# A 96-row weight load cut into fourteen loads of falling row counts, at the end of a decode kernel

## The chip, the cores and the metric

The kernel runs on one core of one Trainium2 chip. The metric is the device time of one execution in microseconds (us); lower is better. Three timed runs of the kernel before gave 190.89, 191.10 and 191.25 us; the median is 191.1 us.

## The reference, cut to what matters

One token (a row of 512 numbers) goes through two branches, which a gate then mixes. Branch A is attention with 32 heads over a cache of 4,096 keys and values. Branch B is a small dense network, whose second weight matrix is `w2` with 1,376 rows of 512 numbers.

```
h   = x @ w1 + b1                  # 512 -> 1376
h   = relu(h) ** 2
b   = h @ w2 + b2                  # 1376 -> 512; w2 is [1376, 512], bf16
a   = attention(x @ wq, k_cache, v_cache) @ wo
out = g * a + (1 - g) * b          # g = sigmoid(sum(x * gate_w))
```

The change concerns only how the last 96 of the 1,376 rows of `w2` (1376 = 10 * 128 + 96) come from device memory.

## The kernel before, in words

**Loads.** Nearly all loads are issued on one queue, that of SyncE (SP), in an order written out by hand in `ORDER` and the loop that starts at L265. The 32 heads are taken four at a time, so keys and values come as eight loads each of 4 MB (`load_kv`, L230). The last values load (V7) comes in four parts of 1 MB, each with a semaphore of its own. Between them stand `wq` (L223), `w1` (L273), four parts of `wo` (`load_wo`, L250, 1 MB each), and the five parts of `w2` (`load_w2`, L258). `W2_PARTS` (L65) names the five parts: two of four groups of 128 rows (512 KB each), then the rest of 96 rows (96 KB), then two of one group of 128 rows (128 KB each). The first part is issued ahead of V7. The other four stand at the very end of the queue, behind the last part of `wo`, in the order L277 to L280: the second four groups, the 96 rows, a group, a group. A DMA of up to 128 rows is spread over the core's 16 DMA engines, which each work through their own share of the queue in order. A DMA adds 16 to its semaphore in all.

**Where the rows go.** The 96 rows land in their own tile `w2b` (L104), the 1,280 others in `w2a` (L100). Until the last head group's scores are done, `w2a` also serves as the scratch tile of the products on VectorE, which is why the first part waits at L267.

**The end on TensorE.** After the last values have landed, TensorE runs this order, which L631 to L642 write out: the first part of `w2` (`mlp_out(0)`, L633), the transposes of the last attention rows (`turn`, `spread`), the last part of `wo` (`out_rows(1)`, L636), and then `mlp_out(1)` to `mlp_out(4)`. Each `mlp_out(c)` first waits for its part's semaphore (L535) and then issues four matmuls for every group of rows. All add into the same accumulator `acc`. Then VectorE adds the bias (L752), TensorE transposes (L642), VectorE copies (L754), and SP stores the 1 KB result with a DMA of four rows (L282), for which L757 waits. ScalarE issues four small loads at the start (L322 to L325): `x`, `gate_w` and `b1` as one row each, and `b2` as four rows.

Of the kernel before, what the change touches and what calls it, by code (L numbers as in the profile page):

```python
# [5 lines left out]
def bass_gated_mix__gqa_block_cached__dense_activation_squared_relu__decode_kernel(  # L6
# [24 lines left out]
    F = 1376  # L31
    FG = 10
# [29 lines left out]
    V_SLOT = [2 + q % 2 for q in range(NQ)]  # L62
    V_PARTS = [[4]] * (NQ - 1) + [[1, 1, 1, 1]]
    QF = 4
    W2_PARTS = [(0, 4), (4, 8), (FG, FG + 1), (8, 9), (9, 10)]  # L65


# [12 lines left out]
    with ctx:  # L80
        def sb(name, shape, dt):
            return ctx.enter_context(nc.sbuf_tensor(name, shape, dt))
# [4 lines left out]
        def sem(name):  # L87
            return ctx.enter_context(nc.semaphore(name))
# [15 lines left out]
        w2b = sb("w2b", [FR, DM], bf16)  # L104
# [49 lines left out]
        acc4 = pO[0:4, 128:192].bitcast(bf16)  # L154
        QR = [pQ[:, :]] + [p[:, :].bitcast(fp32) for p in KP[0:3]] + [pQ[:, :]] * (NQ - QF)
        H = KP[0][:, 0:2 * (FG + 1)].bitcast(fp32)
# [7 lines left out]
        s_w1 = sem("s_w1")  # L164
        s_w2 = [sem(f"s_w2{n}") for n in range(len(W2_PARTS))]
        s_wo = [sem(f"s_wo{g}") for g in range(2)]
# [61 lines left out]
        @block.sync  # L228
        def _(eng):
            def load_kv(n):  # L230
                kind, q = ORDER[n]
                if q >= 2:
                    done(kind, q - 2)
                if kind == "K":
                    eng.dma_start(KV[:, K_SLOT[q], :], k_q[q, :, :]).then_inc(s_k[q], 16)
                else:
                    at = 0
                    for m, sv in zip(V_PARTS[q], s_v[q]):
                        a, b = at * PB * 128, (at + m) * PB * 128
                        eng.dma_start(KV[:, V_SLOT[q], a:b], v_q[q, :, a:b]).then_inc(sv, 16)  # L240
                        at += m

            def done(kind, q):
                if kind == "K":
                    eng.wait_ge(s_sd, NP * (q + 1))
                    eng.wait_ge(s_t, GQ * (q + 1))
                else:
                    eng.wait_ge(s_pv, q + 1)

            def load_wo(g):  # L250
                if g == 0:
                    eng.wait_ge(s_qps, NQ)
                elif g < NG - 1:
                    eng.wait_ge(s_wd, g)
                a = 0 if g < NG - 1 else 1
                eng.dma_start(wo_sb[:, a, :, :], wo_v[g, :, :, :]).then_inc(s_wo[a], 16)

            def load_w2(n):  # L258
                a, b = W2_PARTS[n]
                if a < FG:  # L260
                    eng.dma_start(w2a[:, a:b, :], w2_v[:, a:b, :]).then_inc(s_w2[n], 16)
                else:
                    eng.dma_start(w2b[:, :], B_w2[FG * 128:F, :]).then_inc(s_w2[n], 16)

            for n in range(len(ORDER)):  # L265
                if n == len(ORDER) - 1:
                    eng.wait_ge(s_sd, NP * NQ)  # L267
                    load_w2(0)
                load_kv(n)
                if n == 2:  # L270
                    eng.wait_ge(s_z, 1)
                    eng.wait_ge(s_b2, 1)
                    eng.dma_start(w1_sb[:, :, :], w1_v[:, :, :]).then_inc(s_w1, 16)  # L273
                if n in WO_AT:
                    load_wo(WO_AT[n])
            load_wo(NG - 1)
            load_w2(1)  # L277
            load_w2(2)
            load_w2(3)
            load_w2(4)  # L280
            eng.wait_ge(s_f4, 1)
            eng.dma_start(out[0, 0, :].rearrange("(j p) -> j p", p=128), fin4[:, :]).then_inc(s_out, 16)  # L282
# [38 lines left out]
        def _(eng):  # L321
# [9 lines left out]
            def qb_copy(c):  # L331
                eng.wait_ge(s_qps, c + 1)
                for r in range(R):
                    eng.activation(qb[rows(r), c, :], QR[c][rows(r), r * 128:(r + 1) * 128], ACT.Copy)\  # L334
                       .then_inc(s_qb, 1)

            def qcol_copy(c):
                eng.wait_ge(s_q, c + 1)
                eng.activation(qcol[:, 4 * c:4 * c + 4], QR[c][:, 0:4], ACT.Copy).then_inc(s_qc, 1)
# [37 lines left out]

            for c in range(QF):
                qb_copy(c)
            for c in range(QF):  # L380
                qcol_copy(c)
# [22 lines left out]
        def _(eng):  # L404
# [32 lines left out]
            def q_rows(c):  # L437
                if c >= QF:
                    eng.wait_ge(s_qc, c)
                for t in range(4):  # L440
                    mm = eng.matmul(QR[c], xb[:, t, :], wq_sb[:, t, c * 512:(c + 1) * 512],  # L441
                                    start=(t == 0), stop=(t == 3))
                mm.then_inc(s_qps, 1)

            def q_cols(c):
                eng.wait_ge(s_qb, R * (c + 1))
                eng.matmul(QR[c][:, 0:4], qb[:, c, :], ident[:, 0:128:32], start=True, stop=True).then_inc(s_q, 1)
# [84 lines left out]
                mm.then_inc(s_wd, 1)  # L532

            def mlp_out(c, last=False):
                eng.wait_ge(s_w2[c], 16)  # L535
                a, b = W2_PARTS[c]
                for n in range(a, b):
                    M = 128 if n < FG else FR
                    w = w2a[:, n, :] if n < FG else w2b[:, :]
                    for j in range(4):  # L540
                        mm = eng.matmul(acc[:, j:j + 1], w[:, j * 128:(j + 1) * 128], hs[0:M, n:n + 1],  # L541
                                        start=False, stop=last, skip_group_check=True)
                if last:
                    mm.then_inc(s_acc, 1)
# [48 lines left out]
            eng.wait_ge(s_xb, 4)  # L593
            for c in range(QF):
                q_rows(c)
            for c in range(QF):
                q_cols(c)
# [33 lines left out]
            at("end")  # L631
            eng.wait_ge(s_hs, 2)
            mlp_out(0)  # L633
            turn()
            spread()
            out_rows(1)  # L636
            mlp_out(1)
            mlp_out(2)
            mlp_out(3)
            mlp_out(4, last=True)  # L640
# [145 lines left out]
```

## Time and profile before

| what | value |
|---|---|
| timed runs | 190.89, 191.10, 191.25 us; median 191.1 |
| the profiled execution's own time | 190.93 us |
| its span (first to last instruction) | 189.6 us |
| around the span | 1.3 us |
| TensorE busy | 138.7 us (73%) |
| VectorE busy | 123.0 us (65%) |
| ScalarE busy | 115.9 us (61%) |
| bytes moved by DMA, mean rate | 78.47 MB, 414 GB/s |
| share of the SP queue's packets in the time of 16 DMA engines | 97.1% |
| granted TensorE clock, mean | 0.725 (0.50 from 164 us to the end) |

How to read it: the span is the time from the first to the last instruction of the profiled execution, and the time of an execution is a little longer. An engine's busy time is a share of the whole span, and says little about one stage. For this change the last 8 us matter, in which the last loads land and TensorE adds them up. A packet is one DMA engine's move of one contiguous row; a 4-byte packet behind a load's rows is that engine's step of the load's semaphore.

### The profile page before, as it was taken

The numbers are of one execution on the slowest core, as the hardware profiler recorded it, in microseconds if no ns is written. First come the engines' busy times: TensorE is split into PE (matmuls) and PEld (weight loads), VectorE is DVE, ScalarE is ACT, GpSimd is POOL, SyncE is SP. The second block draws the span as 40 slices with busy tenths as digits, with TensorE's granted clock in tenths as the row PEclk, the third lists the DMA queues.
The fourth block names the chain that finished last, engine by engine and source line by source line (L and its number), as shares of the span: only waits on it lengthen the run. The fifth ranks groups of instructions, "written<-read, shape, count | busy, mean of one in ns | idle before, by whom it ended". The sixth has DMA issues, their size and how long they took to land. (4 is left out here: it accounts for less than half of the span.)

```text
span 189.6 us, 6235 instructions
## 1 busy us (share of the span) xinstructions
PE 138.7 (73%) x2688; PEld 120.8 (64%) x2688; DVE 123.0 (65%) x123; ACT 115.9 (61%) x242; POOL 6.0 (3%) x13
## 2 busy tenths in 40 slices
PE   0009587668849979969968797929867596899855
PEld 0003265536739779959958695829766595789854
DVE  1100099979969999996997299819990599701011
ACT  3004659948989985985987099709962298560000
POOL 4000000000700000000000000000000000000000
PEclk9999969958975965795795569555975589555555
DMA  6999999989999999999999999999999999999991
GB/s 218 443 443 442 443 442 425 429 374 481 425 387 422 442 443 439 430 436 429 429 430 422 422 429 436 442 443 442 404 446 429 422 411 432 444 387 422 420 389 62
DMA packets 4321, 78.47 MB, mean 414 GB/s; under 512 B 499, under 2 KB 853, under 8 KB 1110
## 3 DMA queue, kind: packets, MB, share of 16 engines
q1 hardware_dynamic: 4296, 78.32, 97.1%
q8 instruction: 7, 0.11, 0.2%
q14 instruction: 4, 0.03, 0.0%
q10 hardware_dynamic: 14, 0.01, 0.0%
HBM read 78.32 MB, written 0.00 MB: 413 GB/s over the span
## 5 line engine op out<-in xcount | busy, mean ns | idle before, releaser
L351 ACT ACTIVATE kT<-KP 128x1024 bf16<-128x1024 bf16 x80 | 75.4, 1041 | 25.2 <-PE KP L456 25.0
L681 DVE TENSOR_TENSOR w2a<-KV,qb 128x1536 f32<-128x1536 bf16 x32 | 56.3, 1760 | 18.3 <-DMA KV<-in_A_k_cache_dram 18.0
L456 PE MATMUL KP<-ident,KV 128*128 128x128 bf16 x640 | 60.0, 256 | 9.2 <-PEq L451 9.1
L456 PEld LDWEIGHTS KP<-ident,KV 128*128 128x128 bf16 x640 | 48.9, 117 | 12.6 <-issue 11.7
L685 DVE TENSOR_REDUCE S<-w2a 128x12 f32<-128x1536 f32 x32 | 56.1, 1753 | 1.1
L463 PE MATMUL pS<-qc,kT 128*128 128x4 bf16 x640 | 28.0, 166 | 13.0 <-PEq L451 11.2
L463 PEld LDWEIGHTS pS<-qc,kT 128*128 128x128 bf16 x640 | 24.7, 99 | 18.6 <-issue 17.3
L497 PEld LDWEIGHTS pO<-E,KV 128*128 128x128 bf16 x1024 | 29.4, 105 | 1.5 <-issue 1.5
L497 PE MATMUL pO<-E,KV 128*128 128x4 bf16 x1024 | 28.5, 166 | 1.4 <-PEq L451 1.4
L368 ACT ACTIVATE E<-S,nM 32x128 bf16<-32x128 f32 x32 | 18.5, 579 | 0.9
L441 PE MATMUL pQ<-W,xb 128*128 128x512 bf16 x20 | 7.8, 531 | 12.5 <-DMA W<-in_A_wq_dram 11.4
L334 ACT ACTIVATE qb<-pQ 32x128 bf16<-32x128 f32 x20 | 5.4, 268 | 14.2 <-PE pQ L441 13.9
L441 PEld LDWEIGHTS pQ<-W,xb 128*128 128x128 bf16 x20 | 2.2, 125 | 14.9 <-DMA W<-in_A_wq_dram 11.5
L357 ACT ACTIVATE S<-pS 32x80 f32<-32x80 f32 x32 | 7.3, 228 | 4.8 <-PE pS L463 4.2
L660 DVE TENSOR_SCALAR e<-ez 128x1 f32<-128x1 f32 x1 | 0.2, 154 | 14.1 <-ACT ez L383 14.1
L368 ACT ACTIVATION_READ_ACCUMULATOR E<-S,nM 32x1 f32 x32 | 8.1, 252 | 0.0
L704 DVE RECIPROCAL rden<-pO 128x4 f32<-128x4 f32 x8 | 1.4, 174 | 9.8 <-PE pO L497 9.8
L493 PE MATMUL pO<-RS,onesf 128*128 128x4 f32 x16 | 4.3, 339 | 1.8 <-PEq L451 1.8
L484 PE MATMUL pM<-identf,mp 128*1 128x128 f32 x8 | 3.0, 372 | 3.2 <-PEq L451 2.9
L493 PEld LDWEIGHTS pO<-RS,onesf 128*128 128x128 f32 x16 | 3.8, 297 | 2.1 <-issue 2.0
L441 PE MATMUL KP<-W,xb 128*128 128x512 bf16 x12 | 4.9, 591 | 0.0
L718 DVE TENSOR_SCALAR hr<-KP 128x10 f32<-128x10 f32 x1 | 0.2, 170 | 6.8 <-PE KP L509 6.8
(74 smaller groups left out, 70.1 us busy)
## 6 DMA issues: line engine op xcount, KB each, us to landing
KV<-in_A_k_cache_dram SPq DMA_DIRECT2D x8, 4096.0 KB, 22.1
KV<-in_A_v_cache_dram SPq DMA_DIRECT2D x7, 4096.0 KB, 28.9
W<-in_A_wq_dram SPq DMA_DIRECT2D x1, 4096.0 KB, 13.6
W<-in_A_wo_dram SPq DMA_DIRECT2D x4, 1024.0 KB, 17.2
KV<-in_A_v_cache_dram SPq DMA_DIRECT2D x4, 1024.0 KB, 13.2
w_sb<-in_B_w_dram SPq DMA_DIRECT2D x1, 1376.0 KB, 23.6
w2a<-in_B_w_dram SPq DMA_DIRECT2D x2, 512.0 KB, 13.9
w2a<-in_B_w_dram SPq DMA_DIRECT2D x2, 128.0 KB, 18.7
```

What stands on the lines that cost most here:

```text
L334: eng.activation(qb[rows(r), c, :], QR[c][rows(r), r * 128:(r + 1) * 128], ACT.Copy)\
L351: eng.activation(kT[:, n % NT, :], KP[n % NKP][:, :], ACT.Copy).then_inc(s_ev, 1)
L357: eng.activation(S[rows(r), q % NS, 0:YQ], S2[rows(r), :, r], ACT.Copy).then_inc(s_cp, 1)
L368: eng.activation(E[rows(r), q % 2, :, r], S[rows(r), q % NS, :], ACT.Exp, bias=nM[rows(r), q:q + 1], scale=SCALE, accum_out=RS[rows(r), q ...
L441: mm = eng.matmul(QR[c], xb[:, t, :], wq_sb[:, t, c * 512:(c + 1) * 512], start=(t == 0), stop=(t == 3))
L456: mm = eng.transpose(KP[(GQ * a + g) % NKP][:, y * 128:(y + 1) * 128], key(a, b), ident[:, :])
L463: mm = eng.matmul(pS[:, R * c:R * c + R], kT[:, (GQ * a + g) % NT, y * 128:(y + 1) * 128], qc2[:, a, :], start=True, stop=True)
L484: eng.transpose(MT, mp[:, a:a + 1], identf[:, :]).then_inc(s_mt, 1)
L493: eng.matmul(DEN[a], onesf[:, :], RS[:, a, :], start=True, stop=True)
L497: mm = eng.matmul(O[a], KV[:, V_SLOT[a], b * 128:(b + 1) * 128], E[:, a, COLUMN[b], :], start=(b == 0), stop=(b == NB - 1))
L681: eng.tensor_tensor(prod, KV[:, K_SLOT[q], x:x + XB * 128].rearrange("p (b d) -> p b d", d=128), qb[:, q, :].unsqueeze(1).to_broadcast([12 ...
L685: eng.tensor_reduce(S[:, q % NS, c:c + XB], prod, AX.X, ALU.add).then_inc(s_sd, 1)
```

## The change

`load_w2(2)` issued one load of 96 rows. It now issues fourteen, of 13, 12, 11, 10, 9, 8, 7, 6, 5, 4, 3, 2, 1 and 5 rows, one behind the other on the same queue, at the same place in its order. All add to the same semaphore, and the wait on TensorE ahead of the four matmuls of `w2b` goes from 16 to 16 * 14 = 224. The rows, their bytes and their place in `w2b` stay the same; nothing else is edited. In the order of instructions, only SP's list grows (by 13 DMAs, between the second and the fourth part of `w2`); those of the other engines are the same.

```diff
+    W2B_PARTS = list(range(13, 0, -1)) + [5]
     W2_PARTS = [(0, 4), (4, 8), (FG, FG + 1), (8, 9), (9, 10)]
...
                 if a < FG:
                     eng.dma_start(w2a[:, a:b, :], w2_v[:, a:b, :]).then_inc(s_w2[n], 16)
                 else:
-                    eng.dma_start(w2b[:, :], B_w2[FG * 128:F, :]).then_inc(s_w2[n], 16)
+                    at = 0
+                    for k in W2B_PARTS:
+                        eng.dma_start(w2b[at:at + k, :], B_w2[FG * 128 + at:FG * 128 + at + k, :])\
+                           .then_inc(s_w2[n], 16)
+                        at += k
...
             def mlp_out(c, last=False):
-                eng.wait_ge(s_w2[c], 16)
+                eng.wait_ge(s_w2[c], 16 * (len(W2B_PARTS) if c == 2 else 1))
```

## The prediction

> **What bounds the kernel now.** I read the chain that ended last first, then the timeline of the last 7 us, then the DMA share in the same stretch, then the trace's records of single packets and landings.
>
> ```profile
> ## 4 chain that ended last, share of the span: by engine, by line
> PE 1%; DVE 0%; issue 0%
> PE pQ L530 1%; PE pQ L541 0%; PE pO L642 0%; DVE fin L754 0%; DVE accs L752 0%
> ```
>
> The chain reaches back only to 185.8 us and names no DMA: at the very end TensorE runs through `out_rows` (L530) and `mlp_out` (L541) without a stall. The timeline of that end (start, duration, engine, line):
>
> ```profile
> 182.47 0.94 PEld L497 LDWEIGHTS pO<-E,KV 128*128 128x128 bf16 x32 [1.50 <-issue]
> ...
> 186.68 0.50 PEld L541 LDWEIGHTS pQ<-hs,w2a 128*128 128x128 bf16 x16
> 187.10 0.18 PEld L541 LDWEIGHTS pQ<-hs,w2b 96*128 96x128 bf16 x4
> 187.21 0.29 PEld L541 LDWEIGHTS pQ<-hs,w2a 128*128 128x128 bf16 x8
> ```
>
> The last values land at 182.32 (landing records) and the weights of their first matmul are loaded at 182.47: 0.15 us from landing to start. From there to the last row it is TensorE's and VectorE's own work. So the end hangs on the last part of V7, which stands ahead of everything that the change touches. The loads behind it have slack. By the landing records: second part of w2 186.33 (needed 186.68), `w2b` 186.53 (187.10), fourth part 186.83 (187.21), fifth part 187.15 (its first weight load is the fifth of the eight, 187.32). The slack is 0.35, 0.57, 0.38 and **0.17 us**. The fifth part is the one that the change can make late: it is queued behind the fourteen loads.
>
> The DMA engines do not finish together. The stretches (us of PE, PEld, DVE, ACT, POOL; then TensorE's clock, DMA share, GB/s):
>
> ```profile
> 184.40:184.80 0.40, 0.02 (x1) 0.05 (x2) 0.21 (x1) 0.00 (x0) 0.00 (x0) 0.50 0.90 300
> 184.80:185.20 0.40, 0.40 (x16) 0.40 (x16) 0.00 (x0) 0.00 (x0) 0.00 (x0) 0.50 0.61 233
> 185.20:185.60 0.40, 0.15 (x6) 0.06 (x3) 0.17 (x1) 0.00 (x0) 0.00 (x0) 0.50 0.48 177
> 185.60:186.00 0.40, 0.15 (x6) 0.18 (x7) 0.00 (x0) 0.00 (x0) 0.00 (x0) 0.50 0.53 184
> 186.00:186.40 0.40, 0.40 (x21) 0.40 (x19) 0.00 (x0) 0.00 (x0) 0.00 (x0) 0.50 0.37 128
> 186.40:186.80 0.40, 0.40 (x21) 0.40 (x19) 0.00 (x0) 0.00 (x0) 0.00 (x0) 0.50 0.06 21
> ```
>
> The share falls to a half at 185.2, stays there to 186, and is that of one engine at the end: half of the engines are a microsecond ahead of the others.
>
> **Which engines are late.** Packets of one engine follow each other closely (1,024 bytes: 46 ns long, a new one every 42 ns; the 4-byte semaphore packet holds up the next row by 6 ns), so the trace's records can be linked into 16 chains, each with its 8 rows and one semaphore step of every load (6 rows of `w2b`). Eight chains end at 184.6 to 185.0, eight at 185.9 to 186.75. The late ones are, but for one, those that carried an instruction fetch of 16 KB (about 1 us each) or several of 8 KB (0.31 us each); the last of all has three of 8 KB. The small loads at the start number some of them. `x`, `gate_w` and `b1` are one row each and their packets lie on one chain, call it engine 0; it ends early, at 185.0. The four rows of `b2` lie on that chain and three more, which I take for engines 1 to 3: they end at 184.8, 185.9 and **186.75**. The last engine of all is one of these three. Chains that run within a few ns of each other can be exchanged; that of engine 0 has a nearly as good reading as a late one (186.4).
>
> **The change part by part.**
>
> 1. *Rows per engine.* `b2` and the store at the end put n rows on n engines. So I take a load of n rows to use engines 0 to n-1, one row each. Engine 0 then gets 14 of the 96 rows, engine 1 13, engine 2 12, engine 3 11, engine 4 10, and so on down to 1 for engine 12 and none for 13 to 15, where each had 6. In step with the rows it gets semaphore packets, where each had one. In ns: engine 0 +8 * 42 + 13 * 6 = +414; engine 1 +7 * 42 + 12 * 6 = +366; engine 2 +318; engine 3 +270; engine 4 +222; engine 8 -18; engines 13 to 15 -258. What stands behind it on the same engine, parts four and five of w2, moves by as much.
> 2. *What that does to the end.* Engine 0 may lose 0.41 us unseen if it is early: it ends 1.7 us ahead of the last. The late engine among 1 to 3 goes from 186.75 by 0.27 to 0.37, middle 0.32. The landing of the fifth part goes from 187.15 to 187.47, and its first weight load from 187.32 to 187.47 + 0.15 = 187.62: **+0.30 us**, ends +0.25 and +0.35. Four matmuls and the unchanged tail follow.
> 3. *The cost of a further load on an engine.* Bounds: 6 ns (a semaphore packet between two rows, as in step 1) and 0.42 us (the time from the last semaphore packet, 186.73, to its landing, 187.15), if each load had to land before the next may start. A gain below 6 ns is out, for the rows keep their size. I take 6 ns, since the semaphore steps of parts three to five follow each other on one engine in 0.34 us, less than the 0.42 that each takes to land, and the row behind a step starts 6 ns later: they overlap.
> 4. *SP's issues.* These are the rows:
>
> ```profile
> 167.54 0.44 SPq L263 DMA_DIRECT2D w2b<-in_B_w_dram  x1
> 168.03 1.87 SPq L261 DMA_DIRECT2D w2a<-in_B_w_dram  x2
> 188.39 0.33 SPq L282 DMA_DIRECT2D out_dram<-fin  x1
> ```
>
>    Thirteen more issues at 0.47 from start to start (V7's four take 1.75 with their gaps) are 6.1 us; the bounds are 0.22 (`gate_w` from ScalarE) and 1.33 us (the second of the two at 168.03: 1.87 less 0.50 and the gap). Behind them wait parts four and five on SP, and then the store, which waits for its data until 188.15. Part five is issued at 168.6 + 6.1 = 174.7 instead, and its rows' turn comes after 184. The cover is 9 us of V7 and `wo` still in the queue, so this costs nothing.
> 5. *The wait for 224* on TensorE is one wait as before. Behind it stand the 12 last matmuls. `w2b` itself lands at most 0.4 us later, inside its slack of 0.57.
>
> Sum: 190.93 + 0.30 = 191.23 for the profiled execution. The median shown is 0.17 above that execution, so I forecast 191.1 + 0.30 = **191.4 us**.
>
> The Trainium skill (DMA: Bandwidth & Descriptors, section Why a DMA increments its semaphore by 16 and not by 1) says that such a load runs on the largest number of engines up to 16 that divides its rows, the lowest-numbered ones. The `b2` packets agree as far as they go (one row on one engine, four rows on four); no run before shows 13 or 11 rows.
>
> **The rivals.** About 0.2% (0.38 us) is what a measurement of this kernel can tell from no change.
>
> - *No delay at all: the last engine is not among 1 to 3, or the run's slack is larger.* For it: the chains were linked by a few ns, and the fetches that make engines late fall as TensorE's program goes; the other seven late chains end by 186.5 and could take +0.22. Against it: the three 8 KB fetches and the `b2` row stay on one chain in the best linking. Time 191.1.
> - *Slower: a short load costs its engine more than a semaphore packet.* The mechanism is the ordering of semaphore steps behind rows, thirteen times within a microsecond on one engine, where the trace never shows more than two of an engine under way. The place is engines 0 to 3, in front of part five. It decides from little: engine 2 has 11 further steps, and 0.38 - 0.30 = 0.08 us more needs only 7 ns each above the 6. At 50 to 100 ns each the end moves by 0.30 + 0.5 to 1.0, to 191.9 to 192.4. At the full 0.42 engine 0 has 14 * 0.47 = 6.6 us for its rows instead of 0.26, 6.3 later; less its lead of 1.7 that is about 4.6, 195.7. Against it: step 3. The Trainium skill (same page, Rules for kernel authors) holds that transfers under 64 KB pay mostly overhead and should be joined, and its fixed cost of about 2 us each would, one after another, make 28 us. The trace speaks against such a series: the last four loads land 0.2 to 0.3 us apart.
> - *Slower: SP is late.* It takes 14 issues of 1.33 us to bring parts four and five to 186.2 and later; the store needs 1.2 us from issue to landing, a 128-row load 0.3 more, so part five lands at about 188.1 and the end comes 0.9 later: 192.0. It decides from some 1.25 us an issue. Only one issue took that long, with nine loads ahead of it; the others and the four-row store took 0.33 to 0.50.
> - *Faster.* TensorE waits for none of these loads in the profile, so lighter engines 13 to 15 gain nothing unless runs without a profile have the fifth part late; at most some 0.25 us came back, 190.85.
>
> **How the numbers follow.** My forecast (0.25 to 0.35 later) has 0.42, of which 0.07 goes over the 0.2% with the timing's own spread. No delay has 0.18 (0.03 of it read as faster). A dearer short load has 0.28, a late SP 0.07, faster 0.05. So slower by over 0.2% is 0.07 + 0.28 + 0.07 = 0.42, faster 0.08, within 0.2% 0.50. The range goes from 190.9 (no delay, less the spread of runs) to 192.4 (100 ns a step, and the late SP inside it); the 0.42 us a step is left out.
>
> **What would show it.** In the profile after: SP's fourteen issues at L267 of 0.2 to 0.5 us each, done by 175 us; the packets of `w2b` on 13 engines at most; the fifth part landing at 187.4 to 187.5; and a gap of about 0.3 us on TensorE ahead of the last four matmuls of L541 (its line in the kernel after is L547), the chain then naming a DMA there. No gap means that the last engine is a high-numbered one. A gap over 0.5 us means that a short load has a price of its own; issues over 1.2 us mean that SP is late.

## The result, and the profile after

The changed kernel takes 192.71 us (median of 4 runs, 192.35 to 192.78) against 191.15 us for the kernel before (4 runs): ratio 1.0081, 95% interval 1.0069 to 1.0093. It is 1.6 us slower. The forecast was 191.4 us, and the range ended at 192.4. The profiled execution of the changed kernel has a span of 191.4 us, 1.8 above the 189.6 of before.

The chain of the profile after, where before's named no DMA:

```profile
## 4 chain that ended last, share of the span: by engine, by line
DMA 9%; SPq 4%; PE 2%; issue 1%; DVE 0%
DMA w2b<-in_B_w_dram 9%; SPq L267 2%; PE pO L503 2%; SPq L242 1%; PE pQ L547 0%; SPq L263 0%; SPq L258 0%; PE pO L499 0%; PE pO L648 0%; DVE fin L760 0%; DVE accs L758 0%
```

The end now hangs on the landing of `w2b` and of the two parts behind it. The timeline of the same kernel shows where TensorE stands still (start, duration, engine, line; in brackets the idle time ahead and its releaser):

```profile
182.52 0.94 PEld L503 LDWEIGHTS pO<-E,KV 128*128 128x128 bf16 x32 [1.55 <-issue]
...
186.73 0.50 PEld L547 LDWEIGHTS pQ<-hs,w2a 128*128 128x128 bf16 x16
186.75 0.56 PE L547 MATMUL pQ<-hs,w2a 128*128 128x1 bf16 x16
188.78 0.18 PEld L547 LDWEIGHTS pQ<-hs,w2b 96*128 96x128 bf16 x4 [1.55 <-DMA w2b<-in_B_w_dram]
188.79 0.26 PE L547 MATMUL pQ<-hs,w2b 96*128 96x1 bf16 x4 [1.47 <-DMA w2b<-in_B_w_dram]
188.96 0.36 PEld L547 LDWEIGHTS pQ<-hs,w2a 128*128 128x128 bf16 x8
```

Up to 186.7 all is as before, to 0.05 us: V7 is not touched. Nearly all of the loss is the gap ahead of the four matmuls of `w2b`, which start at 188.78 instead of 187.10. Two short waits add the rest: the first weights of parts four and five are loaded at 188.96 and 189.13, each 0.04 us behind the landing of its part. VectorE's bias, which follows the last matmul, starts at 189.44 instead of 187.63, 1.81 later. The DMA share by stretches (the last two columns are the share and GB/s) shows something odd about that gap:

```profile
186.40:186.80 0.40, 0.40 (x21) 0.40 (x19) 0.00 (x0) 0.00 (x0) 0.00 (x0) 0.50 0.10 15
186.80:187.20 0.40, 0.40 (x20) 0.40 (x17) 0.00 (x0) 0.00 (x0) 0.00 (x0) 0.50 0.06 5
187.20:187.60 0.40, 0.12 (x5) 0.03 (x2) 0.00 (x0) 0.00 (x0) 0.00 (x0) 0.50 0.07 23
187.60:188.00 0.40, 0.00 (x0) 0.00 (x0) 0.00 (x0) 0.00 (x0) 0.00 (x0) 0.50 0.19 46
188.00:188.40 0.40, 0.00 (x0) 0.00 (x0) 0.00 (x0) 0.00 (x0) 0.00 (x0) 0.50 0.00 0
188.40:188.80 0.40, 0.01 (x1) 0.02 (x2) 0.00 (x0) 0.00 (x0) 0.00 (x0) 0.50 0.00 0
```

The last packet of any load begins at 187.71, and TensorE waits for a load until 188.78. (The view counts a packet where it begins. The 46 GB/s of 187.6 to 188.0 are mostly one instruction fetch of 16 KB, which runs from 187.70 to 188.82. It is not what TensorE waits for: the kernel before has such a fetch at 187.59 without a wait, and the experiment own_sems below has none there and still starts `w2b` at 188.78.) What is missing is not data but steps of the semaphore. The trace's landing records, which give the time at which each step arrives, say so directly. The last steps of `w2b`, then the last of the fourth and the fifth part (us):

```
after:  w2b ... 187.866  188.041  188.216  188.392  188.567  188.742   part 4: 188.918   part 5: 189.092
before: w2b                                                   186.526   part 4: 186.825   part 5: 187.149
```

From one step to the next it is 174 to 176 ns, seven times in a row, also where eight rows lie between two steps (part 4 to part 5).

Linking the packets into chains again, engine by engine, gives for the 16 engines 14, 13, 12, 11, 10, 8, 7, 6, 5, 4, 3, 2, 1, 0, 0 and 0 rows of `w2b`. The chain of 14 rows is that of the small one-row loads (engine 0), and it is early: its last packet is at 186.02. The chain of 13 rows (engine 1) carries the three 8 KB fetches and is the last. On it the thirteen loads pass at 48 ns each at first (185.79 to 186.42). Then four rows of part 4 take 173 to 188 ns instead of 46, and the last packet is at 187.71. Its landing follows 1.38 us behind, where it was 0.42 before. As in the prediction, chains that run close together can be exchanged, so this linking supports the reading and does not prove it alone.

**The theory.** An engine's semaphore steps land about 175 ns apart at the closest. A burst of short loads puts steps on it faster than that; they queue, and with enough of them open (their packet has passed, their landing has not come) the rows behind are held too. Only the engine that is last counts: engine 1, with 13 loads. The main rivals: the rows' number (A, the forecast's 6 ns a step); many rows on one engine or many short loads, wherever they lie (A'); SP's issues (B); many steps on one semaphore (C); bytes (E). Further rivals stand with the experiment that tests them.

### The profile page after: what moved, and what is told of

It reads as the page before. It is cut to its first block, busy times and chain, and to the rows that moved or that the text cites. A ratio compares the mean times of both kernels' runs of the same rounds, so it can differ in the third digit from the quotient of the medians.

```text
span 191.4 us, 6245 instructions
## 1 busy us (share of the span) xinstructions
PE 136.5 (71%) x2685; PEld 118.8 (62%) x2688; DVE 123.0 (64%) x123; ACT 115.7 (60%) x242; POOL 6.0 (3%) x13
## 5 line engine op out<-in xcount | busy, mean ns | idle before, releaser
L462 PE MATMUL KP<-ident,KV 128*128 128x128 bf16 x640 | 58.2, 251 | 10.2 <-PEq L457 10.2
L462 PEld LDWEIGHTS KP<-ident,KV 128*128 128x128 bf16 x640 | 47.2, 114 | 14.0 <-issue 12.8
L469 PEld LDWEIGHTS pS<-qc,kT 128*128 128x128 bf16 x640 | 24.2, 98 | 19.6 <-issue 17.8
L447 PE MATMUL pQ<-W,xb 128*128 128x512 bf16 x17 | 6.7, 527 | 13.8 <-DMA W<-in_A_wq_dram 12.3
L515 PE MATMUL KP<-xcol,w_sb 128*128 128x1 bf16 (+1 forms) x44 | 4.4, 204 | 0.0
```

The source lines that it names most:

```text
L462: mm = eng.transpose(KP[(GQ * a + g) % NKP][:, y * 128:(y + 1) * 128], key(a, b), ident[:, :])
L469: mm = eng.matmul(pS[:, R * c:R * c + R], kT[:, (GQ * a + g) % NT, y * 128:(y + 1) * 128], qc2[:, a, :], start=True, stop=True)
L515: mm = eng.matmul(H[0:M, n:n + 1], lhs, xcol[:, t:t + 1], start=False, stop=(t == 3))
```

## The experiments

Every kernel below has the change's form of the load; only the list of row counts or the lines shown differ. All were compared with the kernel before on the same chip.

**six16: steps without skew.**

```diff
-    W2B_PARTS = list(range(13, 0, -1)) + [5]
+    W2B_PARTS = [16] * 6
```

> The 96 rows as six loads of 16 rows: every engine has 6 rows of w2b as before, but 6 semaphore steps in place of one. Theory (an engine's semaphore steps land no closer than 175 ns, and engine 1 is the last): on engine 1 the eight steps behind the second part of w2 take 8 * 0.175 = 1.40 us from its landing, so the fifth part lands at 187.75 instead of 187.15 and the end comes about 0.4 to 0.5 us later (0.25%). Rival A (a step costs 6 ns, the rows' number per engine decides): 0.03 us, no change. Rival B (SP's issues are late): 5 more issues, all done by 172 us, no change.

Measured: 191.55 us against 191.13, ratio 1.0015 (0.9997 to 1.0032). The interval just includes no change, but the profile shows the wait:

```profile
187.44 0.18 PEld L547 LDWEIGHTS pQ<-hs,w2b 96*128 96x128 bf16 x4 [0.35 <-DMA w2b<-in_B_w_dram]
187.44 0.27 PE L547 MATMUL pQ<-hs,w2b 96*128 96x1 bf16 x4 [0.27 <-DMA w2b<-in_B_w_dram]
```

TensorE starts `w2b` at 187.44, 0.04 behind its last landing. The last landings are 187.400 (`w2b`), 187.575 and 187.750: 175 ns apart again, and the theory had 187.75 for the last. The bytes and rows of every engine are those of before. By rival A the last landing would have moved by 0.03 us; it moved by 0.60. Rival A falls.

**one_row and two_row: the same burst on engine 0 alone, and on engines 0 and 1.**

```diff
-    W2B_PARTS = list(range(13, 0, -1)) + [5]
+    W2B_PARTS = [80] + [1] * 8 + [8]          # one_row
+    W2B_PARTS = [80] + [2] * 8                # two_row
```

> One load of 80 rows, eight of one row and one of 8 rows (10 loads): engine 0 has 14 rows and 10 steps, engine 1 has 6 rows and 2 steps. Theory: engine 0 is early; its 12 steps from 184.2 us on end at 186.4, ahead of engine 1; no change, within 0.1 us of before. Rival A' (14 rows on one engine, or ten short loads, cost wherever they are): 0.4 to 1.3 us later. Rival B (SP's issues): the same as two_row.

> One load of 80 rows and eight of two rows (9 loads): engines 0 and 1 have 13 rows and 9 steps each, the others 5 rows and one step. Theory: engine 1 is the last, its 11 steps behind the second part of w2 take 1.93 us, so the fifth part lands at about 188.3 and the end comes 1.0 us later (0.5%). Rival A (rows and 6 ns a step): 0.3 us later. Rival B (SP's issues): as one_row, which has one load more.

Measured: one_row 190.92 us, ratio 0.9985 (0.9965 to 1.0005), no difference shown. two_row 192.04 us, ratio 1.0040 (1.0020 to 1.0059), slower. The lines of `w2b` on TensorE, first one_row:

```profile
187.15 0.18 PEld L547 LDWEIGHTS pQ<-hs,w2b 96*128 96x128 bf16 x4
187.18 0.24 PE L547 MATMUL pQ<-hs,w2b 96*128 96x1 bf16 x4
```

and two_row:

```profile
188.00 0.18 PEld L547 LDWEIGHTS pQ<-hs,w2b 96*128 96x128 bf16 x4 [0.85 <-DMA w2b<-in_B_w_dram]
188.01 0.27 PE L547 MATMUL pQ<-hs,w2b 96*128 96x1 bf16 x4 [0.77 <-DMA w2b<-in_B_w_dram]
```

Ten loads cost nothing, nine cost 0.9 us. This is the pair that decides: fourteen rows and ten steps on the early engine pass unseen; nine steps on the last engine do not. Rivals A' and B fall: the run without a loss has one issue on SP more than the other.

**own_sems: a semaphore for each of the fourteen loads.**

```diff
+        s_w2b = [sem(f"s_w2b{i}") for i in range(len(W2B_PARTS))]
...
-                    for k in W2B_PARTS:
+                    for i, k in enumerate(W2B_PARTS):
...
-                           .then_inc(s_w2[n], 16)
+                           .then_inc(s_w2b[i], 16)
...
-                eng.wait_ge(s_w2[c], 16 * (len(W2B_PARTS) if c == 2 else 1))
+                for sm in s_w2b if c == 2 else [s_w2[c]]:
+                    eng.wait_ge(sm, 16)
```

> The fourteen loads of the changed kernel, each with a semaphore of its own, TensorE waits for all fourteen. Theory (the limit is the engine's): landings on the last engine stay 175 ns apart, the end 1.5 to 1.9 us later than before, as the changed kernel. Rival C (the limit lies in many steps of one semaphore): the landings come together, and about 0.3 us is left, with up to 0.7 us for thirteen more waits on TensorE.

Measured: 193.37 us, ratio 1.0114 (1.0070 to 1.0158). The last landing of each load, in the order of issue (13 rows down to 1, then 5):

```
13: 186.465   12: 186.635   11: 186.805   10: 186.985   9: 187.164   8: 187.363   7: 187.550
 6: 187.742    5: 187.914    4: 188.084    3: 188.253   2: 188.433   1: 186.818   5: 188.611
```

Each lands 169 to 199 ns behind the one ahead of it, though no two share a semaphore. The exception explains itself: the load of one row lies on engine 0 alone, and that is done at 186.818. So rival C falls. Nor is the limit one for the whole core: landings of one and the same load, which come from different engines, lie as close as 6 ns (184.181 and 184.187 for the load of 13 rows). The limit is the engine's. The median is 2.2 us above before, more than the 1.5 to 1.9 expected, and 0.3% above the changed kernel. Most of that lies outside the span: the spans of the four runs are 191.3 to 191.7 us, where the changed kernel's are 191.0 to 191.4. Its cause was not tried, and the intervals overlap. The numbers of landing records are 14, 13, 12 and so on to 2 for the loads of 13 to 1 rows: one for each row and one at the issue.

**half: the fourteen loads with half the bytes.**

```diff
+                    eng.dma_start(w2b[:, 0:256], B_w2[FG * 128:F, 0:256]).then_inc(s_w2[n], 16)
                     at = 0
                     for k in W2B_PARTS:
-                        eng.dma_start(w2b[at:at + k, :], B_w2[FG * 128 + at:FG * 128 + at + k, :])\
+                        eng.dma_start(w2b[at:at + k, 256:512], B_w2[FG * 128 + at:FG * 128 + at + k, 256:512])\
...
-                eng.wait_ge(s_w2[c], 16 * (len(W2B_PARTS) if c == 2 else 1))
+                eng.wait_ge(s_w2[c], 16 * (len(W2B_PARTS) + 1 if c == 2 else 1))
```

> One load of all 96 rows with their first 256 columns, and the fourteen loads with the other 256 columns: the fourteen move half as many bytes, engine 1 has one semaphore step more than in the changed kernel (14 for w2b). Theory (the step sets the pace, not the bytes): 16 steps of 175 ns behind the second part of w2 on engine 1, the fifth part lands at 189.1 and the end comes 1.8 to 2.0 us later than before (1.0%). Rival E (the pace is set by a load's bytes): half the price, about 0.9 us later.

Measured: 192.94 us, ratio 1.0096 (1.0077 to 1.0116). The last six landings of `w2b` are 175 to 176 ns apart, with 512 bytes a step as with 1,024. The fifth part lands at 189.42 where the theory had 189.1; in this run the second part of w2, from which the theory counts, is itself 0.19 later than in before (186.52). Rival E falls.

**early14: the burst ahead of V7.**

```diff
                     load_w2(0)
+                    load_w2(2)
...
             load_w2(1)
-            load_w2(2)
             load_w2(3)
```

> The fourteen loads are issued behind the first part of w2, ahead of V7, instead of near the end; w2b is then there long before TensorE needs it. Theory (an engine with too many open steps holds up its rows, as the packets of the changed kernel show for engines 0 and 1, and nothing gives the time back): the last part of V7 lands 0.9 to 1.3 us later on engine 1, and so does the end (0.5 to 0.7%). Rival D (only the landing of the steps is slow, the rows pass at 48 ns a load): 0.6 us later. Rival F (only who waits for these loads pays): no change.

Measured: 192.67 us, ratio 1.0089 (1.0070 to 1.0108). The timeline of its end:

```profile
184.14 0.94 PEld L503 LDWEIGHTS pO<-E,KV 128*128 128x128 bf16 x32 [1.55 <-issue]
...
188.77 0.18 PEld L547 LDWEIGHTS pQ<-hs,w2b 96*128 96x128 bf16 x4
```

Nothing waits for `w2b` here, and the loss is the same: the last part of V7 lands at 183.98 instead of 182.32, 1.66 us later, and the tail starts later by as much. The packets show why: rows of 8 KB, nearly all of which took about 0.31 us before (one took 0.86, behind an instruction fetch), take up to 1.29 us between 170.3 and 174.8. The direction is the theory's, but its size, 0.9 to 1.3 us, was too small: with rows of V7 behind them the thirteen loads on engine 1 cost 1.66 / 13 = 0.13 us each. Rivals D (0.6) and F (none) fall.

**skew3 and engine0: the skew without the burst, and 36 rows on engine 0.**

```diff
-    W2B_PARTS = list(range(13, 0, -1)) + [5]
+    W2B_PARTS = [39, 33, 24]                  # skew3
+    W2B_PARTS = [64, 31, 1]                   # engine0
```

> The 96 rows as three loads of 39, 33 and 24 rows: engines 0 to 10 get 8 rows and 3 steps each, engine 11 5 rows, engine 12 3 rows, engines 13 to 15 none. Nearly the skew of the changed kernel with few steps. Theory: engine 1 has 2 rows and 2 steps more than before, the fifth part lands 0.1 us later, inside TensorE's slack; no change within 0.15 us. Rival A'' (the skew of rows itself is the price): at least 0.5 us later.

> The 96 rows as loads of 64, 31 and 1 rows: 64 rows lie on 16 engines, 4 each, and loads of 31 and 1 rows on engine 0 alone, which gets 36 rows and 3 steps. Theory (engine 0 ends 1.7 us ahead of engine 1): its 30 further rows of 42 ns (1.27 us) pass unseen, engine 1 has 2 rows less, the fifth part lands 0.08 us earlier and TensorE, which did not wait for it, ends at the same time: no change to 0.1 us faster. Rival G (engine 0 is not early): 0.9 us later. If a load of 31 rows lies on 31 or 16 engines, its landing count shows it and the run tells nothing of engine 0.

Measured: skew3 190.91 us, ratio 1.0001 (0.9990 to 1.0012); engine0 191.02 us, ratio 0.9999 (0.9989 to 1.0008). Neither differs from the kernel before, so rival A'' falls too. In engine0 the three loads have 20 landing records, 16 for the load of 64 rows and 2 each for those of 31 and 1 rows, so the 31 rows did lie on one engine. It takes 30 rows more and nobody waits: engine 0 is early, rival G falls. The fifth part lands at 187.15 as before, not 0.08 earlier as expected. In skew3 it lands at 187.23, 0.08 later than before, inside the slack.

**The steps counted.** On the last engine, from the last landing of the second part of w2 to the last of `w2b`:

| kernel | steps of w2b on engine 1 | us | us a step |
|---|---|---|---|
| before | 1 | 0.195 | 0.195 |
| skew3 | 3 | 0.574 | 0.191 |
| six16 | 6 | 1.112 | 0.185 |
| two_row | 9 | 1.643 | 0.183 |
| changed | 13 | 2.347 | 0.181 |
| half | 14 | 2.550 | 0.182 |

The time grows with the steps alone: from 3 to 14 steps by (2.550 - 0.574) / 11 = 0.18 us each, over rows of 512 and 1,024 bytes and one to six rows a step. That the steps of one engine land at this pace, and not faster, when a burst comes is shown; what in the chip sets it, and whether each step waits for its own rows, stays open.

No version beat the kernel before. That fits: there TensorE waits for none of the late loads, so a better order of them has nothing to give back.

## Why the prediction was wrong, point by point

- *What bounds the kernel, and the slack* were right. V7 ends at the same time, and the only new wait is at the parts behind it.
- *Which engines are late* was right: engine 0 early, engine 1 the last, as one_row, two_row and engine0 show.
- *Step 1, rows per engine,* was right to the row (14, 13, 12, 11, 10, 8 ... 0). The Trainium skill's rule on the number of engines (DMA: Bandwidth & Descriptors, section Why a DMA increments its semaphore by 16 and not by 1) agrees: the landing counts of own_sems show 13 to 1 engines, and the 31 rows of engine0 went to one.
- *Step 3, the cost of a further load on an engine,* is the step that failed. I took 6 ns, the time that a step's packet takes away from the rows, because the steps overlapped. They do overlap, but only to one landing in about 175 ns. In before no engine had step packets closer than 0.26 us (six rows and a step; the closest landings of the last engine are 0.195 apart), so the trace never asked for more than it could give, and I read a packet's cost as the cost of the whole step. With 13 steps on engine 1 the landing of the fifth part moves from 187.15 to 189.09, 1.94 us, where I had 0.32. Less the 0.13 that the slack covers (0.17, of which 0.04 is left from landing to start), that is the 1.81 us of the profile.
- *The rival with the right mechanism* was the dearer short load, with its place (ahead of part five) right. Its price was outside of what I counted: I let 50 to 100 ns a step into the range and left out all the rest to 0.42 us, though nothing in the trace spoke for 100 rather than 175. The bounds of step 3 were 6 ns and 0.42 us, and the range should have kept the upper one.
- *The choice of engine 0 in that rival* was wrong. At the full 0.42 us a step the prediction let engine 0 set the end (195.7), though engine 1 has nearly as many steps and no lead of 1.7 us to use up. At the measured pace the lead of engine 0 hides its 14 steps, and engine 1 decides.
- *Step 2, the end,* follows step 3. Engine 1's last packet came 0.98 us later (186.73 to 187.71), not 0.27 to 0.37: four rows took some 0.13 us more each. The other 0.96 is its landing, which follows 1.38 instead of 0.42 behind.
- *Step 4, SP,* was right: fourteen issues of 0.25 to 0.59 us, the two behind them done by 174.3, nothing late.
- *Step 5, the wait,* was wrong in its cover: `w2b` lands 2.2 us later, not 0.4 within its slack of 0.57, and the gap is ahead of the last twelve matmuls, not the last four.

The Trainium skill calls the semaphore write's bubble tiny and the write essentially free (same page, section Anatomy of one DMA — SWDGE (gpsimd) path, which is on loads that GpSimd issues; those here are issued by SyncE). For a step behind many rows the traces agree (6 ns between rows). For a burst of short loads the measured 175 ns a step decides.

## What to carry to other kernels

A load costs each engine that carries it a semaphore step, and here these land no faster than about one in 175 ns, which is the time of about four rows of 1 KB. So count steps per engine as well as bytes: by that estimate (175 / 42), many loads in a row that give an engine fewer than some four such rows each are paced by their steps. Look for the engine that is last, not for the mean: ten short loads on an early engine were free, nine on the last one cost 0.9 us. And when a price has bounds far apart because the trace never went that fast, keep the whole distance in the range.

## What the runs showed of the hardware that was not expected

- In a burst, steps of one engine land about 175 ns apart in these runs (174 to 176 at the end of the changed kernel, 169 to 199 in own_sems), on one semaphore or on fourteen, with 512 or 1,024 bytes each.
- Rows behind such a burst are held: in the changed kernel rows of 1 KB took up to 0.21 us (in before 0.046 for most, 0.092 at most), in early14 rows of 8 KB up to 1.29 us instead of 0.31. That the open steps are what holds them fits, and no run shows it by itself.
- In engine0 SP was held far longer than by any other issue: 7.63 us for the two issues behind the load of 31 rows on one engine. That this load is the reason was not tried. It cost nothing, since the rows of these two loads were not due for some seven more microseconds:

```profile
167.57 1.35 SPq L267 DMA_DIRECT2D w2b<-in_B_w_dram  x3
168.97 7.63 SPq L263 DMA_DIRECT2D w2a<-in_B_w_dram  x2
```
